# Spreading w_down over 128 partitions, and wo's fourth group in 14 small DMAs, in a one-core decode kernel

## The chip, the core and the metric

One core of a Trainium2 chip runs the whole program. Time is device time in microseconds (us), the median of several executions. Inputs and output are in the chip's main memory; the core computes from its on-chip memory, whose 128 partitions are filled by DMA.

## The reference

One token passes through attention over a cache of 65,536 positions in 32 heads and, beside it, through a gated feed-forward block; a learnt scalar gate mixes the two. All inputs are bfloat16.

```
def _A_ref(x, k_cache, v_cache, wq, wo):        # caches: 1 x 32 x 65536 x 128
    q = (x @ wq).reshape(B, Sq, H, Dh)...        # x: 1 x 1 x 512
    scores = einsum("bhqd,bhkd->bhqk", q, k_cache) * (Dh ** -0.5)
    p = softmax(scores)
    o = einsum("bhqk,bhkd->bhqd", p, v_cache)
    return o...reshape(B, Sq, H * Dh) @ wo       # wo: 4096 x 512
def _B_ref(x, w_gate, w_up, w_down):             # w_down: 1792 x 512
    return (silu(x @ w_gate) * (x @ w_up)) @ w_down
g = sigmoid((x * gate_w).sum(-1))
return g * a + (1 - g) * b
```

The two caches are 1,074 MB of the 1,088 MB that are read.

## The kernel before

**Tiles and ring.** Each head's K and V are cut into four tiles of 16,384 positions, 4 MB each (32 KB on each of 128 partitions). There are 128 K tiles and 128 V tiles; K0, V0 and so on are their numbers here. They share one ring of five buffers (`SLOTS = 5`, tag `big`) with `wq_t`, `gu_t` (w_gate and w_up), `wd_t` (w_down) and, at the end, `wo_t` (the second half of wo). A load into a ring buffer is issued when the last reader of its old content is done.

**Order of work.** The list `steps` pairs the K tile to be scored with the V tile to be summed; V runs four to eight tiles behind K. In each step the queue of SyncE (SP) issues the load of K tile n, then small loads, then the load of V tile v. VectorE multiplies the K tile by the query and folds it from 128 to 16 columns (`products`, L240 and L244). TensorE adds up those columns (`scores`, L254), multiplies the probabilities by the V tile in 32 matmuls (`values`, L302), and projects a finished head by its 128 rows of wo (`project`, L335). The softmax's small steps lie between.

**Feed-forward.** Its three parts run in steps 1 to 3 (`feed_forward_in`, `_mid`, `_out`). w_down is held on 64 partitions with 28 rows of 1 KB each. `hT`, the hidden vector on 128 partitions, is moved to 64 partitions by two matmuls into `h_ps` and a copy to `h2`, and 28 matmuls (L209) then sum into `b_ps`. The ring buffer of `wd_t` is next used by K5, so K5's load waits for the last of these matmuls.

**Who loads w_down and wo.** `load_wd` issues eight DMAs of eight partitions each (L146): two at the start, behind gate_w, and six in step 2, behind K2. wo's first half (heads 0 to 15) comes in four groups of four heads (`load_wo`, L167), each one DMA of 128 partitions by four pieces of 1 KB, into a pool of two buffers. Group 0 is loaded in step 3, groups 1, 2 and 3 in front of V8, V24 and V40. Head 12 is the first to use group 3; it is projected in the step of V52. wo's second half comes behind V127 in five DMAs (`load_wo_end`, L161) of 4, 4, 4, 2 and 2 heads.

**The end.** V126 is loaded in two parts, V127 in five (32, 32, 32, 16 and 16 of 128 columns). After V127's matmuls come the projections of heads 16 to 19, the last head's column (`head_column`, L323) and the projections of heads 20 to 31; then `a_ps` is copied and written out (L413, L414).

Of the kernel before, what the change touches and what calls it, by code (L numbers as in the profile page):

```python
# [8 lines left out]
ACT = mybir.ActivationFunctionType  # L9
ALU = mybir.AluOpType  # L10
AXIS = mybir.AxisListType
P = 128
# [13 lines left out]
def kernel(  # L26
# [14 lines left out]
    nc = tc.nc  # L41
    bf16 = mybir.dt.bfloat16
    f32 = mybir.dt.float32

    _, H, Sk, Dh = A_k_cache.shape
    D = A_x.shape[2]
    F = B_w_gate.shape[1]
    KT = D // P
    FT = F // P
    G = Sk // (NB * P)  # L50
# [6 lines left out]
    consts = ctx.enter_context(tc.tile_pool(name="consts", bufs=1))  # L57
# [3 lines left out]
    wo_pool = ctx.enter_context(tc.tile_pool(name="wo_pool", bufs=2))  # L61
# [3 lines left out]
    psum_m = ctx.enter_context(tc.tile_pool(name="psum_m", bufs=2, space=bass.MemoryType.PSUM))  # L65
# [3 lines left out]
    def big(name):  # L69
        return ring.tile([P, NB * Dh], bf16, name=name, tag="big")  # L70
# [12 lines left out]
    ident_b = consts.tile([P, P], bf16, name="ident_b")  # L83
# [18 lines left out]
    def load(dst, cache, n, name, cuts=(0, NB)):  # L102
        h, g = divmod(n, G)
        t = big(name)
        view = t.rearrange("p (j d) -> p j d", d=Dh)
        src = cache[0, h, g * NB * P : (g + 1) * NB * P, :].rearrange("(p j) d -> p j d", j=NB)
        for a, b in zip(cuts[:-1], cuts[1:]):
            nc.sync.dma_start(out=view[:, a:b, :], in_=src[:, a:b, :])
        dst[n] = view
# [25 lines left out]
    nc.sync.dma_start(out=wgu_sb[:, 1], in_=B_w_up.rearrange("(p t) f -> p t f", t=KT))  # L135
    wd_t = big("wd_t")
    HP = P // 2
    GT = F // HP
    wd_sb = wd_t[:HP, : GT * D].rearrange("p (t n) -> p t n", t=GT)
    wd_rows = B_w_down.rearrange("(p t) n -> p t n", t=GT)  # L140

    def load_wd(*which):
        for i in which:
            lo = (0, 1, 2, 3, 32, 33, 34, 35)[i]
            part = slice(lo, lo + 29, 4)
            nc.sync.dma_start(out=wd_sb[part], in_=wd_rows[part])  # L146

    with nc.allow_non_contiguous_dma(reason="small"):
        nc.sync.dma_start(out=gwT, in_=gate_w.rearrange("(p t) -> p t", t=KT))
# [1 line left out]
    WG = 4  # L151
    wo_tiles = {}

    WH = H // 2
    wo_end = []

    def load_wo_end(cuts):
        t = big("wo_t")[:, : (H - WH) * D].rearrange("p (h n) -> p h n", n=D)
        rows = A_wo[WH * P :, :].rearrange("(h p) n -> p h n", p=P)
        for a, b in zip(cuts[:-1], cuts[1:]):  # L160
            nc.sync.dma_start(out=t[:, a:b, :], in_=rows[:, a:b, :])  # L161
        wo_end.append(t)

    def load_wo(g):
        wo_tiles[g] = wo_pool.tile([P, WG, D], bf16, name="wo_sb")
        rows = A_wo[g * WG * P : (g + 1) * WG * P, :]
        nc.sync.dma_start(out=wo_tiles[g], in_=rows.rearrange("(h p) n -> p h n", p=P))  # L167

    def feed_forward_in():

# [18 lines left out]
    def feed_forward_mid(gu_sb, eg):  # L189
        nc.vector.tensor_scalar_add(eg, eg, 1.0)  # L190
        nc.vector.reciprocal(eg, eg)
        hprod = consts.tile([P, FT], f32, name="hprod")
        nc.vector.tensor_tensor(out=hprod, in0=gu_sb[:, :FT], in1=eg, op=ALU.mult)
        hT = consts.tile([P, FT], bf16, name="hT")
        nc.vector.tensor_tensor(out=hT, in0=hprod, in1=gu_sb[:, FT:], op=ALU.mult)
        xg = consts.tile([P, KT], f32, name="xg")
        nc.vector.tensor_tensor(out=xg, in0=xT, in1=gwT, op=ALU.mult)
        xs = consts.tile([P, 1], f32, name="xs")
        nc.vector.tensor_reduce(out=xs, in_=xg, axis=AXIS.X, op=ALU.add)
        h_ps = psum_m.tile([HP, GT], f32, name="h_ps", tag="misc")  # L200
        for r in range(2):
            nc.tensor.matmul(
                h_ps[:, r * FT : (r + 1) * FT], lhsT=ident_b[:, r::2], rhs=hT, start=True, stop=True
            )
        h2 = consts.tile([HP, GT], bf16, name="h2")
        nc.scalar.activation(out=h2, in_=h_ps, func=ACT.Copy)
        b_ps = psum_m.tile([1, D], f32, name="b_ps", tag="misc")
        for t in range(GT):
            nc.tensor.matmul(  # L209
                b_ps, lhsT=h2[:, t : t + 1], rhs=wd_sb[:, t, :], start=(t == 0), stop=(t == GT - 1)  # L210
            )
        g_ps = psum_m.tile([P, 1], f32, name="g_ps", tag="misc")
        nc.tensor.matmul(g_ps, lhsT=ones_f, rhs=xs, start=True, stop=True)
        eg2 = consts.tile([P, 1], f32, name="eg2")
        nc.scalar.activation(out=eg2, in_=g_ps, func=ACT.Exp, scale=-1.0)
        return b_ps, eg2
# [13 lines left out]
    def products(n, a=0, b=NB):  # L230

        h = n // G
        K = K_tiles[n][:, a:b, :]
        qb = q_bc[:, h * Dh : (h + 1) * Dh]
        q_rep = bass.AP(
            tensor=qb.tensor,
            offset=qb.offset,
            ap=[list(qb.ap[0]), [0, b - a], [1, Dh]],
        )
        yield nc.vector.tensor_tensor(out=K, in0=K, in1=q_rep, op=ALU.mult)  # L240
        half = Dh
        while half > WIDTH:
            half //= 2
            yield nc.vector.tensor_tensor(  # L244
                out=K[:, :, 0:half], in0=K[:, :, 0:half], in1=K[:, :, half : 2 * half],
                op=ALU.add,
            )
# [15 lines left out]
    def row_max(h):  # L263

        m = small.tile([P, 1], f32, name="m")
        nc.vector.tensor_reduce(out=m, in_=S_tiles[h], axis=AXIS.X, op=ALU.max)  # L266
        diag = small.tile([P, P], f32, name="diag")
        nc.scalar.activation(out=diag, in_=ident_f, func=ACT.Copy, scale=m)  # L268
        mT_ps = psum_m.tile([P, P], f32, name="mT_ps", tag="misc")
        nc.tensor.matmul(mT_ps, lhsT=ones_f, rhs=diag, start=True, stop=True)  # L270
        return mT_ps

    def exponentials(h, mT_ps):
        top = small.tile([P, 1], f32, name="top")
        nc.vector.tensor_reduce(out=top, in_=mT_ps, axis=AXIS.X, op=ALU.max)  # L275
        bias = small.tile([P, 1], f32, name="bias")
        nc.scalar.activation(out=bias, in_=top, func=ACT.Copy, scale=-scale)
        P_tiles[h] = ppool.tile([P, NBH], bf16, name="P_sb")
        nc.scalar.activation(  # L279
            out=P_tiles[h], in_=S_tiles[h], func=ACT.Exp, bias=bias, scale=scale,  # L280
            accum_out=rowsum[:, h : h + 1],
        )
        del S_tiles[h]
# [61 lines left out]
    v = 0  # L345
# [9 lines left out]
    for n, v in steps:  # L355
        if n is not None and n > 1:
            load(K_tiles, A_k_cache, n, "K_t")
        if n == 2:
            load_wd(2, 3, 4, 5, 6, 7)
        if n == 3:  # L360
            load_wo(0)
        if v is not None:
            if v % (WG * G) == 2 * G and v // (WG * G) + 1 < WH // WG:
                load_wo(v // (WG * G) + 1)
            load(V_tiles, A_v_cache, v, "V_t", (0, NB) if v < N - 2 else (0, 64, NB) if v < N - 1 else (0, 32, 64, 96, 112, NB))
            if v == N - 1:
                load_wo_end((0, 4, 8, 12, 14, 16))
        if n == 2:
            ff = feed_forward_mid(*ff)
        halves = (0, NB // 2)  # L370
        vector = iter(()) if n is None else products(n)
        if n == 0:
            vector = (i for a in halves for i in products(n, a, a + NB // 2))
        top_of = None
        if n is None:
            top_of = H - 1 if S_tiles else None
        elif n % G == 0 and n > 0:
            top_of = n // G - 1
            vector = (i for a in halves for i in products(n, a, a + NB // 2))
        if top_of is not None:  # L380
            next(vector, None)
            mT_ps = row_max(top_of)
            next(vector, None)
            exponentials(top_of, mT_ps)
        for _ in vector:
            pass
        if n == 1:
            ff = feed_forward_in()
        if n == 3:
            feed_forward_out(*ff)  # L390
        if tot_ps is not None:
            weight(*tot_ps)
            tot_ps = None
        if done is not None:
            head_column(done, head_copy(done))
        if v is not None:
            values(v)
        if top_of is not None:
            tot_ps = top_of, total(top_of)
        if n is not None:  # L400
            scores(n)
        if done is not None and done < WH:
            project(done)
        done = v // G if v is not None and v % G == G - 1 else None
# [40 lines left out]
```

## Time and profile before

| | us |
|---|---|
| median of 3 runs | 2534.66 (2534.63 to 2534.93) |
| the profiled execution | 2534.51 |
| its span (first to last instruction of the program) | 2532.6 |
| 16 DMA engines: share of the span with a packet of the kernel's loads | 99.7% |
| VectorE busy | 2175.5 (86%) |
| TensorE matmul busy | 1742.4 (69%), at a granted clock of 0.749 |
| bytes read | 1087.64 MB, 429 GB/s over the span |

The page gives shares of one execution. Beside it the trace holds a record of every DMA packet, with its start, duration, size and queue, and of every landing, that is, each time one of the 16 DMA engines reports the end of its part of a DMA. A packet is one contiguous piece: 32,768 B for a full K or V tile, 28,672 B for w_down, 1,024 B for wo.

### The profile page before, as it was taken

The page shows a single profiled execution, that of the slowest core. Times are in us where ns is not written, and L with a number is a line of the kernel's source. Part 1 is how long each engine was busy: PE and PEld are TensorE (multiplying, and loading weights), DVE is VectorE, ACT ScalarE, POOL GpSimd, SP SyncE. Part 2 cuts the span into 40 slices and gives each one's busy share as a digit, 9 for nine tenths or more (in the row PEclk, how much of TensorE's full clock was granted, in tenths as well). Part 3 has the DMA queues.
Part 4 walks back from the last instruction along what each step waited for, and adds up shares of the span by engine and source line. Part 5 has one row for each costly group of instructions (what it writes and reads, how often), then busy time and mean ns, then how long its engine had stood idle before and what let it go on. Part 6 is the DMA issues. An engine that isn't in the chain of part 4 may idle for free.

```text
span 2532.6 us, 15260 instructions
## 1 busy us (share of the span) xinstructions
PE 1742.4 (69%) x6738; PEld 712.1 (28%) x6738; DVE 2175.5 (86%) x784; ACT 75.9 (3%) x207; POOL 0.7 (0%) x6
## 2 busy tenths in 40 slices
PE   4677666776677666676776677667666776677679
PEld 2222222222222222222222223222222232222223
DVE  7998888888888999998888888888888888888860
ACT  1000000000000000000000000000000000000000
POOL 0000000000000000000000000000000000000000
PEclk7677777777777676677777777777777777777779
DMA  9999999999999999999999999999999999999998
GB/s 415 433 433 430 433 433 433 432 430 435 432 432 434 431 433 432 432 433 433 432 434 433 432 434 433 432 432 434 432 431 434 433 430 434 434 431 433 434 432 339
DMA packets 42884, 1088.63 MB, mean 430 GB/s; under 512 B 4737, under 2 KB 8834, under 8 KB 9090
## 3 DMA queue, kind: packets, MB, share of 16 engines
q1 hardware_dynamic: 42674, 1087.66, 99.7%
q8 instruction: 53, 0.87, 0.1%
q14 instruction: 13, 0.11, 0.0%
q10 hardware_dynamic: 144, 0.00, 0.0%
HBM read 1087.64 MB, written 0.00 MB: 429 GB/s over the span
## 4 chain that ended last, share of the span: by engine, by line
DMA 68%; PE 22%; DVE 10%; issue 1%; ACT 0%; DVEq 0%; SPq 0%
DMA V_t<-in_A_v_cache_dram 61%; PE O_ps L302 20%; DMA K_t<-in_A_k_cache_dram 5%; DVE K_t L240 5%; DVE K_t L244 5%; PE S_ps L254 1%; DMA wo_t<-in_A_wo_dram 1%; DMA wq_t<-in_A_wq_dram 0%; PE qg_ps L117 0%; DVE m L266 0%; PE oh_ps L323 0%; PE a_ps L335 0%; PE a_ps L227 0%; ACT P_sb L279 0%; DVE top L275 0%
## 5 line engine op out<-in xcount | busy, mean ns | idle before, releaser
L302 PE MATMUL O_ps<-V_t,P_sb 128*4 128x512 bf16 x4096 | 1157.3, 453 | 496.8 <-DMA V_t<-in_A_v_cache_dram 494.3
L240 DVE TENSOR_TENSOR K_t<-K_t,q_bc 128x16384 bf16<-128x16384 bf16 (+1 forms) x160 | 1117.2, 6983 | 254.4 <-DMA K_t<-in_A_k_cache_dram 232.9
L244 DVE TENSOR_TENSOR K_t<-K_t 128x4096 bf16<-128x4096 bf16 (+3 forms) x480 | 1030.9, 2148 | 14.3
L302 PEld LDWEIGHTS <-P_sb 128*4 128x4 bf16 x4096 | 393.9, 97 | 1241.0 <-issue 897.5
L254 PE MATMUL S_ps<-K_t,ident_b 128*128 128x128 bf16 x2048 | 466.0, 394 | 107.0 <-DVE K_t L244 106.9
L254 PEld LDWEIGHTS <-ident_b 128*128 128x128 bf16 x2048 | 227.6, 115 | 330.0 <-issue 140.2
L323 PE MATMUL oh_ps<-ident_f,O_sb 4*128 4x1 f32 x256 | 57.9, 343 | 74.1 <-ACT O_sb L315 74.1
L323 PEld LDWEIGHTS oh_ps<-ident_f,O_sb 4*128 4x128 f32 x256 | 55.2, 314 | 83.7 <-ACT O_sb L315 78.9
L270 PE MATMUL mT_ps<-diag,ones_f 128*128 128x128 f32 x64 | 23.6, 468 | 79.8 <-ACT diag L268 79.8
L268 ACT ACTIVATE diag<-ident_f,m 128x128 f32<-128x128 f32 x32 | 12.8, 401 | 2099.3 <-DVE m L266 2099.3
L317 DVE COPY O_sb<-O_ps 4x256 f32<-4x256 f32 x1 | 0.4, 414 | 52.1 <-ACT O_sb L315 52.1
L270 PEld LDWEIGHTS mT_ps<-diag,ones_f 128*128 128x128 f32 x64 | 14.7, 285 | 95.6 <-ACT diag L268 95.6
L266 DVE TENSOR_REDUCE m<-S_ps 128x1 f32<-128x512 f32 x32 | 21.9, 683 | 7.4 <-PE S_ps L254 7.4
L315 ACT ACTIVATE O_sb<-O_ps 4x512 f32<-4x512 f32 (+1 forms) x32 | 18.1, 566 | 131.0 <-PE O_ps L302 131.0
L279 ACT ACTIVATE P_sb<-S_ps,bias 128x512 bf16<-128x512 f32 x32 | 22.0, 687 | 1.0
L117 PE MATMUL qg_ps<-wq_t,X_bc 128*128 128x512 bf16 x32 | 8.6, 436 | 13.2 <-DMA wq_t<-in_A_wq_dram 13.2
L293 DVE RECIPROCAL recip<-tot_ps 128x1 f32<-128x1 f32 x32 | 5.1, 160 | 12.2 <-PE tot_ps L288 12.2
L209 PE MATMUL b_ps<-wd_t,h 64*1 64x512 bf16 x28 | 12.1, 629 | 4.3 <-DMA K_t<-in_A_k_cache_dram 4.3
L288 PEld LDWEIGHTS tot_ps<-rowsum,ones_f 128*128 128x128 f32 x64 | 9.5, 188 | 14.0 <-issue 14.0
L288 PE MATMUL tot_ps<-rowsum,ones_f 128*128 128x1 f32 x64 | 12.2, 260 | 0.0
L330 ACT ACTIVATE oT<-oh_ps,rg 128x1 bf16<-128x1 f32 x32 | 8.4, 263 | 76.6 <-PE oh_ps L323 76.6
L227 PE MATMUL a_ps<-b_sb,ones_f 1*1 1x512 f32 x2 | 1.9, 1032 | 12.1 <-ACT b_sb L226 12.1
(42 smaller groups left out, 73.8 us busy)
## 6 DMA issues: line engine op xcount, KB each, us to landing
K_t<-in_A_k_cache_dram SPq DMA_DIRECT2D x127, 4096.0 KB, 35.3
V_t<-in_A_v_cache_dram SPq DMA_DIRECT2D x126, 4096.0 KB, 29.1
wq_t<-in_A_wq_dram SPq DMA_DIRECT2D x1, 4096.0 KB
K_t<-in_A_k_cache_dram SPq DMA_DIRECT2D x2, 2048.0 KB, 16.8
V_t<-in_A_v_cache_dram SPq DMA_DIRECT2D x2, 2048.0 KB
V_t<-in_A_v_cache_dram SPq DMA_DIRECT2D x3, 1024.0 KB, 29.4
wo_sb<-in_A_wo_dram SPq DMA_DIRECT2D x4, 512.0 KB, 17.3
gu_t<-in_B_w_gate_dram SPq DMA_DIRECT2D x1, 1792.0 KB
```

Of the source, the lines that this page charges most:

```text
L209: nc.tensor.matmul(b_ps, lhsT=h2[:, t : t + 1], rhs=wd_sb[:, t, :], start=(t == 0), stop=(t == GT - 1))
L240: yield nc.vector.tensor_tensor(out=K, in0=K, in1=q_rep, op=ALU.mult)
L244: yield nc.vector.tensor_tensor(out=K[:, :, 0:half], in0=K[:, :, 0:half], in1=K[:, :, half : 2 * half], op=ALU.add,)
L254: nc.tensor.matmul(S_tiles[h][:, g * NB : (g + 1) * NB], lhsT=ident_b, rhs=K_tiles[n][:, :, c], start=(c == 0), stop=(c == WIDTH - 1),)
L266: nc.vector.tensor_reduce(out=m, in_=S_tiles[h], axis=AXIS.X, op=ALU.max)
L268: nc.scalar.activation(out=diag, in_=ident_f, func=ACT.Copy, scale=m)
L270: nc.tensor.matmul(mT_ps, lhsT=ones_f, rhs=diag, start=True, stop=True)
L279: nc.scalar.activation(out=P_tiles[h], in_=S_tiles[h], func=ACT.Exp, bias=bias, scale=scale, accum_out=rowsum[:, h : h + 1],)
L288: nc.tensor.matmul(tot_ps, lhsT=ones_f, rhs=rowsum[:, h : h + 1], start=True, stop=True)
L302: nc.tensor.matmul(O_tiles[h], lhsT=P_tiles[h][:, g * NB + j : g * NB + j + 4], rhs=V_tiles[n][:, j : j + 4, :], start=(g == 0 and j == 0) ...
L315: nc.scalar.activation(out=O_sb[:, :cut], in_=O_ps[:, :cut], func=ACT.Copy)
L323: nc.tensor.matmul(oh_ps, lhsT=O_sb[:, c * Dh : (c + 1) * Dh], rhs=ident_f[0:4, c : c + 1], start=(c == 0), stop=(c == 3),)
```

## The change

w_down is laid out on 128 partitions with 14 rows each. The eight small DMAs (eight partitions each, the same partitions as before) now carry only the first two rows (`WR = 2`, 2 KB per partition). Two more DMAs follow them in step 2: rows 2 to 13 of all 128 partitions, and rows 0 and 1 of partitions 64 to 127. `hT` is used as it is: the two matmuls and the copy are gone, and `b_ps` is summed by 14 matmuls.

wo's groups 0, 1 and 2 are loaded as before. Group 3 is cut by partitions into 14 DMAs of 3, 5, 6, 7, 9, 10, 11, 12, 13, 14, 15, 16, 4 and 3 partitions (`WP`), one in front of each of V36 to V49.

```diff
     wd_t = big("wd_t")
     HP = P // 2
-    GT = F // HP
-    wd_sb = wd_t[:HP, : GT * D].rearrange("p (t n) -> p t n", t=GT)
-    wd_rows = B_w_down.rearrange("(p t) n -> p t n", t=GT)
+    WR = 2
+    wd_sb = wd_t[:, : FT * D].rearrange("p (t n) -> p t n", t=FT)
+    wd_rows = B_w_down.rearrange("(p t) n -> p t n", t=FT)
 
     def load_wd(*which):
         for i in which:
             lo = (0, 1, 2, 3, 32, 33, 34, 35)[i]
             part = slice(lo, lo + 29, 4)
-            nc.sync.dma_start(out=wd_sb[part], in_=wd_rows[part])
+            nc.sync.dma_start(out=wd_sb[part, :WR, :], in_=wd_rows[part, :WR, :])
...
-    def load_wo(g):
-        wo_tiles[g] = wo_pool.tile([P, WG, D], bf16, name="wo_sb")
-        rows = A_wo[g * WG * P : (g + 1) * WG * P, :]
-        nc.sync.dma_start(out=wo_tiles[g], in_=rows.rearrange("(h p) n -> p h n", p=P))
+    WP = (3, 5, 6, 7, 9, 10, 11, 12, 13, 14, 15, 16, 4, 3)
+
+    def load_wo(g, piece=None):
+        lo, hi = 0, P
+        if piece is not None:
+            lo = sum(WP[:piece])
+            hi = lo + WP[piece]
+        if lo == 0:
+            wo_tiles[g] = wo_pool.tile([P, WG, D], bf16, name="wo_sb")
+        rows = A_wo[g * WG * P : (g + 1) * WG * P, :].rearrange("(h p) n -> p h n", p=P)
+        nc.sync.dma_start(out=wo_tiles[g][lo:hi], in_=rows[lo:hi])
...
-        h_ps = psum_m.tile([HP, GT], f32, name="h_ps", tag="misc")
-        for r in range(2):
+        b_ps = psum_m.tile([1, D], f32, name="b_ps", tag="misc")
+        for t in range(FT):
             nc.tensor.matmul(
-                h_ps[:, r * FT : (r + 1) * FT], lhsT=ident_b[:, r::2], rhs=hT, start=True, stop=True
-            )
-        h2 = consts.tile([HP, GT], bf16, name="h2")
-        nc.scalar.activation(out=h2, in_=h_ps, func=ACT.Copy)
-        b_ps = psum_m.tile([1, D], f32, name="b_ps", tag="misc")
-        for t in range(GT):
-            nc.tensor.matmul(
-                b_ps, lhsT=h2[:, t : t + 1], rhs=wd_sb[:, t, :], start=(t == 0), stop=(t == GT - 1)
+                b_ps, lhsT=hT[:, t : t + 1], rhs=wd_sb[:, t, :], start=(t == 0), stop=(t == FT - 1)
             )
...
         if n == 2:
             load_wd(2, 3, 4, 5, 6, 7)
+            nc.sync.dma_start(out=wd_sb[:, WR:, :], in_=wd_rows[:, WR:, :])
+            nc.sync.dma_start(out=wd_sb[HP:, :WR, :], in_=wd_rows[HP:, :WR, :])
...
-            if v % (WG * G) == 2 * G and v // (WG * G) + 1 < WH // WG:
+            if v % (WG * G) == 2 * G and v // (WG * G) + 2 < WH // WG:
                 load_wo(v // (WG * G) + 1)
+            if 0 <= v - 2 * (WG * G) - G < len(WP):
+                load_wo(WH // WG - 1, v - 2 * (WG * G) - G)
```

## The prediction

> **What bounds the kernel.** I read the page's slices, queues and chain first.
>
> ```profile
> DMA  9999999999999999999999999999999999999998
> ...
> q1 hardware_dynamic: 42674, 1087.66, 99.7%
> q8 instruction: 53, 0.87, 0.1%
> ...
> DMA 68%; PE 22%; DVE 10%; issue 1%; ACT 0%; DVEq 0%; SPq 0%
> ```
>
> The 16 DMA engines never rest, so a change that saves bytes, or shares them out better, is what can move the end. Here the bytes stay; only their shares change. For that a mean over 16 engines is no use. In the trace's packet records each packet starts 3 to 8 ns before the end of the one ahead of it on its engine, and each engine works off SP's loads in order. So I chained the 42,674 packets into 16 rows, one per engine. Steps from one packet to the next: 32,768 B 1209.4 ns, 28,672 B 1058.8, 16,384 B 607.1, 1,024 B 42.35, and 5.85 for the 4-byte packet that ends each DMA's part. They lie on 4.6 ns + 36.77 ps per byte. From K2 to V125 no row has a gap over 0.02 us but at a packet of another queue, and once one of 0.13: no engine ever lacks work.
>
> ```
> end of V127's last packet (us from the span's start), by engine
> 8 engines that carry w_down:    2513.46 2513.54 2513.84 2514.54 2515.93 2519.44 | with fetches: 2522.24 (6)  2523.32 (7)
> 8 engines without w_down:       2506.76 2506.80 | with fetches: 2513.67 (6) 2514.08 (6) 2515.03 (7) 2515.16 (7) 2515.20 (6) 2515.30 (7)
> ```
>
> In brackets are packets of q8, the instruction queue (16 KB each). They go round eight engines in a fixed turn, and each puts its engine back by (2523.32 - 2513.46) / 7 = 1.41 us, or 1.21 on the others. Two engines have both loads, fetches and all of w_down's surplus. The slower one, S below, is the last by 1.08 us, and everything waits for it: a tile is there when its last sixteenth is. That the end hangs on S is seen in VectorE's timeline and the last steps of the chain.
>
> ```profile
> 2436.44 8.69 DVE L240 TENSOR_TENSOR K_t<-K_t,q_bc 128x16384 bf16<-128x16384 bf16 x1 [2.65 <-DMA K_t<-in_A_k_cache_dram]
> ...
> 2504.16 20.87 DMA wo_t<-in_A_wo_dram
> ...
> 2525.07 1.02 PE a_ps L335 x4
> 2526.09 0.98 PE oh_ps L323 x8
> 2527.07 2.69 PE a_ps L335 x12
> ```
>
> VectorE had idled 2.65 us and began K127, the last K tile, 0.09 us after its last landing (2436.34), which is S's. The last landing of wo is at 2529.11, 5.8 us of packets after S's 2523.32, and the matmul that needs it starts at 2529.16.
>
> **The change: w_down.** An engine of the first group had 8 x (1058.8 + 5.85 ns) = 8.52 us. Now it has eight small parts, 8 x (79.9 + 5.85), its eighth of a sixteenth of rows 2 to 13, 8 x 456.4 + 5.85, and four packets of 2 KB: 0.69 + 3.66 + 0.33 = 4.67 us. (79.9 and 456.4 are estimates from the line above; these sizes do not occur before.) So -3.85 us for each of the first group, S among them. The other group had nothing and gets 3.66 + 0.33 = +3.98.
>
> **wo's group 3.** Before, 32 packets on every engine: 32 x 42.35 + 5.85 = 1.36 us. Now a DMA of n partitions gives, I take it, one partition to each of n engines. The row for it: in the packet records w_down's DMAs of eight partitions lie on the same eight engines, one packet each. If those are the lowest-numbered engines each time, engine 0 takes part in all 14 pieces, engine 7 in 8, engine 15 in 1, at 4 x 42.35 + 5.85 = 175 ns each: 2.45 us, 1.40 and 0.18. Against before +1.09, +0.04 and -1.19.
>
> [...]
>
> **Which engine S is.** The turn of the fetches is S, six engines without w_down, the other slow one, and S again. Two neighbours of the first group beside six of the second: engines 6 and 7 (then 8 to 13), or 0 and 1 (with 10 to 15, if the turn runs down). For S the pieces cost +0.04 in the one case, +1.09 in the other. Nothing in the trace decides, so I take the middle for the number and both for the range: S ends 3.85 - 0.04 = 3.81 to 3.85 - 1.09 = 2.76 us earlier, middle 3.3. Who is late next: the second group's latest, 2515.30 + 3.98 + 0.04 = 2519.32 at most, against S's 2519.5 to 2520.6. So S stays the bound, barely.
>
> **SP's queue in step 2.** At the start SP and ScalarE issue eight DMAs at once; the ninth waits for the first, and so on.
>
> ```profile
> SPq L167 <- DMA K_t<-in_A_k_cache_dram: 10.3, 1, 10.3
> ...
> SPq L146 <- DMA xT<-in_A_x_dram: 4.0, 1, 4.0
> SPq L146 <- DMA wq_t<-in_A_wq_dram: 4.0, 1, 4.0
> ```
>
> L167's load is the eighth behind K2 (six of w_down, K3, then it) and was issued at 53.91, 0.49 us behind the end of K2 on S. In the changed order the eighth behind K2 is the second new DMA, and K3 stands behind it: K3's issue moves from 43.20 to about 52.5 (K2 ends on S at 53.42 - 1.96 = 51.46, + 0.49, + one issue of 0.62). From an issue to first packets it takes 1.2 to 2.4 us (wq: 0.74 to 1.95 and 3.13), so K3 starts at 53.7 to 54.9. What hides it is the 3.66 us of rows 2 to 13: an unladen engine is done with w_down at 50.1 + 3.99 = 54.1, S at 51.46 + 4.5 = 55.96. So engines of the second group may idle up to 0.8 us, S none. I take nought for the end and keep 0.8 on the second group for the range: 2519.32 + 0.8 = 2520.1 is still near S.
>
> **The rest, at nothing.** The pieces add 13 issues of about 0.6 us (L146's are 0.62) to SP, in front of V36 to V49, while V's median from issue to landing is 29.1 us. The DMA eight before any of them lies at least five tiles back, whose buffer was already free. Group 3's pool buffer was group 1's, last read in V32's step; its last piece comes with V49 and is needed at V52. Fourteen matmuls of L209 fewer (629 ns), two of L202 and the copy free K5's buffer earlier; K5 was issued 8 us before any engine ran out.
>
> **Sum.** Span 2532.6 - 3.3 = 2529.3; the profiled execution 2534.51 - 3.3 = 2531.2; on the median, 0.15 above it, 2531.35, call it 2531.3. That is 0.13%: within 0.2% of 2534.66, that is 5.07 us, about what a measurement of this kernel can tell from no change. Likeliest case: 2530.85 (S engine 7) to 2531.9 (S engine 0).
>
> **Rivals.** *TensorE sets the tail.* From 2472.6 to the end TensorE has one wait, 1.62 us at 2504.1 for V125. If it cannot start its tail earlier, only that is gained: 2534.66 - 1.62 = 2533.0. For it: the last 25 us are matmuls at 216 ns with slacks of 0.05 to 2 us; a stretch at half clock (it was 0.5 until 2467.1) would double that. Against: the tail hangs on K127's landing, which moves with S. 0.08.
>
> *Odd pieces fall on one engine.* If the split wants a divisor of 16, the rows show no contradiction (eight is one). Then engine 0 alone takes the pieces of 3, 5, 7, 9, 11, 13 and 15 and halves or quarters of the rest: 3+5+3+7+9+5+11+3+13+7+15+1+1+3 = 86 partitions x 4 x 42.35 = 14.6 us, +13.2. If engine 0 is S, the end is 13.2 - 3.85 = 9.4 us later: 2544. Otherwise it decides only where engine 0 comes from behind S: 2513.5 to 2519.4 + 9.4 = 2522.9 to 2528.8 against 2523.3, 2534 to 2540. 0.05.
>
> *Each small DMA costs its engines a pause.* At 1.2 us from issue to packets, unhidden, 14 pieces are 17 us: 2534.66 - 3.3 + 17 = 2548. It would need engines that have run dry between pieces; the records show none in steady state. 0.03. [...]
>
> *More than 5.07 us gained* would need S off the fetches or fewer of them (1.41 each): 0.02.
>
> **Numbers.** Forecast 0.82. Range 2530.4 to 2533.0: down 0.45 from the best end, for the spread of runs and a third of one fetch, up through the tail's rival. Faster by over 0.2%: 0.02. Slower: 0.05 + 0.03 less what of the odd pieces stays inside, 0.07. Within: 0.91.
>
> **What would show it.** Right: packets chained again, S ends V127 at 2519.5 to 2520.6, the second group's engines with fetches close behind, and K3 issued at 52 to 53 behind a wait for K2. Wrong: V127's end on S unmoved, over 8 engines or one with a pile of 1 KB packets between V36 and V49, gaps in the rows, or an end that does not follow S.

## The result and the profile after

The changed kernel takes 2545.61 us (2545.09 to 2546.77, 4 runs) against 2534.64 beside it: ratio 1.0045, 95% interval 1.0032 to 1.0059. It is 11 us slower where 3.3 us less were forecast. The profiled execution took 2546.77, its span 2545.0.

These lines of the profile's page after the change answer to those shown of before; the row of bytes per slice (GB/s) is added.

```profile
span 2545.0 us, 15241 instructions
...
DMA  9999999999999999999999999999999999999998
GB/s 408 429 431 430 430 431 432 429 430 431 432 432 429 427 425 418 427 431 430 432 431 431 431 430 431 433 429 433 431 430 432 431 432 431 432 431 431 431 431 350
...
q1 hardware_dynamic: 43010, 1087.66, 99.7%
q8 instruction: 52, 0.85, 0.1%
...
DMA 70%; PE 22%; DVE 6%; issue 0%; ACT 0%; SPq 0%; DVEq 0%
```

Bytes are the same, the DMA engines are as full as before (99.7%), and the chain has the same shape. So hardly any waiting was added: the engines were busy for longer with the same bytes. The last K tile and the tail show that nearly the whole delay, 11.6 of the 12.4 us between the two spans, is there before the tail (VectorE's timeline, then the chain's last steps; before, VectorE began K127 at 2436.44, and the chain's last DMA step and its last projections began at 2504.16 and 2527.07):

```profile
2448.01 8.69 DVE L240 TENSOR_TENSOR K_t<-K_t,q_bc 128x16384 bf16<-128x16384 bf16 x1 [4.31 <-DMA K_t<-in_A_k_cache_dram]
```

```profile
2516.00 21.15 DMA wo_t<-in_A_wo_dram
2537.20 1.02 PE a_ps L335 x4
2538.22 0.98 PE oh_ps L323 x8
2539.20 2.85 PE a_ps L335 x12
```

Where it builds up is seen when the span is cut at the stage of wo's pieces (V36 to V49). The columns after the times are busy times by engine, the granted clock, the share of DMA and the GB/s. First before, then after:

```profile
700.00:775.00 75.00, 50.12 (x198) 20.63 (x197) 65.04 (x24) 2.12 (x6) 0.00 (x0) 0.77 1.00 433
775.00:1080.00 305.00, 202.19 (x772) 85.20 (x770) 291.92 (x108) 10.19 (x28) 0.00 (x0) 0.70 1.00 432
...
1500.00:2000.00 500.00, 344.00 (x1308) 139.95 (x1305) 434.39 (x156) 14.54 (x41) 0.00 (x0) 0.75 1.00 433
```

```profile
700.00:775.00 75.00, 50.48 (x200) 20.77 (x199) 65.27 (x24) 2.12 (x6) 0.00 (x0) 0.77 1.00 432
775.00:1080.00 305.00, 196.19 (x753) 81.82 (x751) 286.68 (x106) 10.21 (x28) 0.00 (x0) 0.71 1.00 425
...
1500.00:2000.00 500.00, 350.26 (x1315) 140.24 (x1315) 434.19 (x153) 12.70 (x36) 0.00 (x0) 0.75 1.00 431
```

Two things: some GB/s less everywhere, also a thousand microseconds behind the last piece, and a dip among the pieces. The packet records say it more sharply. From 12 us on every undisturbed 32,768 B packet of before lasts 1213 ns (the program's first packets are longer in both kernels). After, the mean is 1213.0 from 12 to 31 us, 1216.8 in 100 to 200 us, 1216.7 in 1500 to 2000, and 1227.3 in 780 to 1080 (packets over 1,400 ns, which stand beside instruction fetches or small packets, left out of these means). The rise is on all 16 engines, and it sets in at about 33 us, in the loads of w_gate and w_up (14,336 B: 535 ns, then 538 to 545), before the first packet of w_down (40.3 us).

### The profile page after: what moved, and what is told of

Its sections match the earlier page's. It is cut to its first block, busy times and chain, and to the rows that moved or that the text cites. A ratio compares the mean times of both kernels' runs of the same rounds, so it can differ in the third digit from the quotient of the medians.

```text
span 2545.0 us, 15241 instructions
## 1 busy us (share of the span) xinstructions
PE 1731.1 (68%) x6722; PEld 707.0 (28%) x6722; DVE 2175.9 (85%) x784; ACT 75.7 (3%) x206; POOL 0.7 (0%) x6
## 3 DMA queue, kind: packets, MB, share of 16 engines
q1 hardware_dynamic: 43010, 1087.66, 99.7%
## 4 chain that ended last, share of the span: by engine, by line
DMA 70%; PE 22%; DVE 6%; issue 0%; ACT 0%; SPq 0%; DVEq 0%
DMA V_t<-in_A_v_cache_dram 63%; PE O_ps L302 21%; DMA K_t<-in_A_k_cache_dram 6%; DVE K_t L240 3%; DVE K_t L244 3%; PE S_ps L254 1%; DMA wo_t<-in_A_wo_dram 1%; PE oh_ps L323 0%; DVE m L266 0%; PE a_ps L335 0%; ACT P_sb L279 0%; PE a_ps L227 0%; PE mT_ps L270 0%; DVE top L275 0%; ACT O_sb L315 0%
## 5 line engine op out<-in xcount | busy, mean ns | idle before, releaser
L323 PEld LDWEIGHTS oh_ps<-ident_f,O_sb 4*128 4x128 f32 x256 | 54.4, 310 | 83.0 <-ACT O_sb L315 78.3
L275 DVE TENSOR_REDUCE top<-mT_ps 128x1 f32<-128x128 f32 x32 | 9.1, 284 | 1.3 <-PE mT_ps L270 1.3
```

The costliest lines, as they stand in the source:

```text
L323: nc.tensor.matmul(oh_ps, lhsT=O_sb[:, c * Dh : (c + 1) * Dh], rhs=ident_f[0:4, c : c + 1], start=(c == 0), stop=(c == 3),)
```

## The experiments

**Is it the kernel, and which part?** First the changed kernel once more, each half of the change alone, and the kernel before.

> The changed kernel once more, unchanged. In its first profile a 32,768 B packet took 1215 to 1222 ns from 33 us on, where the kernel before has 1213 to its end; over some 2,030 packets per engine that is about 8 us. Theory A (the change brings this pace): again 2545 us, and packets of 1213 ns until 33 us, 1215 to 1222 after it. Theory B (the pace is of that execution, from something beside the kernel): packets of 1213 ns and an end near 2531 to 2535 us.

> Only w_down's part of the change; wo's group 3 in one DMA as before. Theory A1 (the new layout of w_down takes away the 8 us by which the first eight engines ran behind the others, and engines in step disturb each other): packets of 1215 to 1222 ns throughout and about +8 - 3.9 = 4 us, 2539 us. Theory A2 (the 14 pieces of wo make the loss): packets of 1213 ns, the slow engine 3.85 us earlier, 2531 us.

> Only wo's part of the change; w_down as before. Theory A1: packets of 1213 ns outside V36 to V49, and a loss of at most the 4 us that V35 to V50 took longer than their packets in the changed kernel: 2535 to 2539 us. Theory A2: the whole loss and more, as w_down's gain is missing: 2545 to 2549 us. By the sum of the prediction alone 2534.8 us.

> The kernel before, with a profile from the same chip as the others. Theory A: packets of 1213 ns to the end and 2534.6 us. Theory B, if what is beside the kernel is still there: packets over 1213 ns here as well, and over 2540 us.

```diff
# w_down only: the change without these lines (group 3 in one DMA again)
-            if v % (WG * G) == 2 * G and v // (WG * G) + 2 < WH // WG:
+            if v % (WG * G) == 2 * G and v // (WG * G) + 1 < WH // WG:
...
-            if 0 <= v - 2 * (WG * G) - G < len(WP):
-                load_wo(WH // WG - 1, v - 2 * (WG * G) - G)
# wo only: before, with WP, load_wo(g, piece) and these lines
-            if v % (WG * G) == 2 * G and v // (WG * G) + 1 < WH // WG:
+            if v % (WG * G) == 2 * G and v // (WG * G) + 2 < WH // WG:
...
+            if 0 <= v - 2 * (WG * G) - G < len(WP):
+                load_wo(WH // WG - 1, v - 2 * (WG * G) - G)
```

| | us | ratio to before, 95% | mean 32 KB packet, 780 to 1080 us | 1500 to 2000 us |
|---|---|---|---|---|
| change again | 2545.62 | 1.0045 [1.003, 1.006] | 1227.3 | 1216.7 |
| w_down only | 2541.71 | 1.0029 [1.0018, 1.0041] | 1217.0 | 1216.8 |
| wo only | 2537.23 | 1.001 [1.0, 1.002] | 1219.3 | 1213.0 |
| before (2534.72 in this batch) | 2534.92, once | | 1213.0 | 1213.0 |

B, a disturbance of one execution, falls: the slower packets come again. So does A2, that the pieces make the whole loss. The pieces make the dip among them and end with it (+2.5 us alone); the w_down half makes the slow packets everywhere, and it alone costs 7 us where it should have gained. A1, that w_down's new shares put the engines in step, was still open, but it has to explain an onset ahead of w_down's first packet.

**What else the w_down half changes.** With `h_ps` and the copy went the tile `h2`. It had 56 bytes on each partition, 64 with padding, and lay ahead of the ring in the on-chip memory. By the sizes of the tiles ahead of it, `wq_t` began at byte 30,976 of each partition (121 x 256) before, and begins at 30,912 (192 beyond a multiple of 256) after; every ring buffer moved with it, since 32 KB is a multiple of 256, and so did wo's buffers and the small tiles, which lie behind the ring. Theory P: this move makes the packets longer. The test puts 64 unused bytes in h2's place, and 192 unused bytes into the kernel before.

```diff
# change and w_down only, with the pad
+    consts.tile([P, 32], bf16, name="pad")
# before, moved
+    consts.tile([P, 96], bf16, name="pad")
# plain w_down, with the pad of 32: no small DMAs, wo as before; in step 2
-            load_wd(2, 3, 4, 5, 6, 7)
-            nc.sync.dma_start(out=wd_sb[:, WR:, :], in_=wd_rows[:, WR:, :])
-            nc.sync.dma_start(out=wd_sb[HP:, :WR, :], in_=wd_rows[HP:, :WR, :])
+            nc.sync.dma_start(out=wd_sb, in_=wd_rows)
```

> The changed kernel with an unused tile of 64 B per partition in the pool of constants. Without it the change puts every later tile 64 B lower, since it no longer has h2 (56 B per partition): the ring's buffers then start 192 B behind a multiple of 256, where before they start on one. Theory P (the place of the ring in a partition sets the packets' pace): 32,768 B packets of 1213 ns throughout, and the end 8 us earlier, 2537 us; what is left over 2531 comes from the pieces between V36 and V49. Theory A1 (engines in step disturb each other): packets of 1215 to 1222 ns and 2545.6 us as without the tile.

> Only w_down's part, with the same 64 B tile. Theory P: packets of 1213 ns, the slow engine 3.85 us earlier, 2531 us, faster than before. Theory A1: 2541.7 us as without the tile.

> The kernel before with an unused tile of 192 B per partition, so that its ring lies 192 B behind a multiple of 256, as in the changed kernel. Theory P: packets of 1215 to 1222 ns from 30 to 50 us on and 8 us more, 2542 to 2543 us. Theory A1: packets of 1213 ns and 2534.7 us.

> w_down in one DMA of 128 partitions behind K2, no small DMAs at all, wo's group 3 in one DMA, with the 64 B tile. Theory P: packets of 1213 ns; each engine has 8 packets of 14,336 B (4.26 us) for w_down, so the slow engine (fetches and half of 8.5 us) gains 4.26 us: 2530.5 us. Theory A1 (all engines in step from the start): packets of 1217 ns or more and 2540 us or later.

| | us | ratio, 95% | 780 to 1080 us | 1500 to 2000 us | V127's last packet ends |
|---|---|---|---|---|---|
| change, pad | 2534.51 | 1.0001 [0.9992, 1.001] | 1220.6 | 1213.0 | 2522.92 |
| w_down only, pad | 2531.81 | 0.9991 [0.9982, 1.0] | 1213.0 | 1213.0 | 2520.84 |
| before, moved by 192 | 2545.07 | 1.0043 [1.0029, 1.0057] | 1217.1 | 1216.8 | 2533.51 |
| plain w_down, pad | 2530.48 | 0.9987 [0.9978, 0.9996] | 1213.0 | 1213.0 | 2519.77 |

(Before: 2534.52 in this batch, V127 2523.32.) P holds in both directions: one unused tile gives the changed kernel 11.1 us back, and one unused tile costs the kernel before 10.5 us, with not one load, wait or matmul changed. P's size was short both times (8 us forecast). A1 falls with it, since w_down's shares are the same with the pad, at 1213.0 ns. An unused tile moves everything that is allocated behind it: these runs don't tell the ring from the rest, nor whether it counts where the loads are written or where the engines read. The same windows, first of before moved by 192, then of the change with the pad:

```profile
700.00:775.00 75.00, 54.79 (x202) 21.75 (x201) 65.28 (x24) 2.12 (x6) 0.00 (x0) 0.73 1.00 432
775.00:1080.00 305.00, 198.13 (x758) 83.04 (x758) 290.80 (x107) 10.20 (x28) 0.00 (x0) 0.70 1.00 431
...
1500.00:2000.00 500.00, 346.94 (x1319) 139.71 (x1317) 434.18 (x152) 12.70 (x36) 0.00 (x0) 0.76 1.00 431
```

```profile
700.00:775.00 75.00, 50.20 (x193) 20.50 (x192) 66.67 (x23) 2.12 (x6) 0.00 (x0) 0.75 1.00 433
775.00:1080.00 305.00, 195.31 (x760) 82.04 (x758) 289.33 (x108) 10.20 (x28) 0.00 (x0) 0.72 1.00 429
...
1500.00:2000.00 500.00, 345.80 (x1309) 140.67 (x1308) 435.84 (x155) 14.82 (x42) 0.00 (x0) 0.75 1.00 433
```

The two effects stand apart: moved, 431 to 432 everywhere and no dip; padded, 433 outside and 429 among the pieces. The GB/s are rounded to whole numbers, and 433 to 431 is 0.5%, so the size is read from times and packets. The moved kernel has 8.1 us more packet time in q1 per engine (2533.22 against 2525.15 in the second run of before), and each of the instruction fetches' 16 KB packets lasts 1064 ns instead of about 930. With seven of them that is 8.1 + 0.9 = 9.0 of the 10.2 us by which V127 ends later. Half of the other 1.2 us is that packets overlap the one ahead less (7.96 us an engine instead of 8.53, summed from 60 to 2500 us); the rest stays without a row.

Plain w_down, one DMA of 128 partitions behind K2 and wo as before, is the fastest version: 4.0 us less than before, and the 95% interval lies below a ratio of 1.

**What makes the pieces cost 2.5 to 2.7 us, and does it matter how far off 256 the ring lies?** With the pad, wo's group 3 was cut in eight DMAs of 8 partitions and one of 64, once with neighbouring partitions in each of the eight, once with every fourth. Packets, sizes and shares are the same in both.

```diff
# the change with the pad; in load_wo, for the piece i (0 to 8, with V36 to V44), cut to the lines on partitions
-            lo = sum(WP[:piece])
-            hi = lo + WP[piece]
# block
+            part = slice(8 * i, 8 * i + 8) if i < 8 else slice(P // 2, P)
# spread
+            lo = (0, 1, 2, 3, 32, 33, 34, 35, 0)[i]
+            part = slice(lo, lo + 29, 4) if i < 8 else slice(P // 2, P)
# before, moved by 64 and by 128
+    consts.tile([P, 32], bf16, name="pad")
+    consts.tile([P, 64], bf16, name="pad")
```

> The changed kernel with the pad, but with wo's group 3 in nine DMAs: eight of 8 neighbouring partitions (0 to 7, 8 to 15, ... 56 to 63, with V36 to V43), then one of partitions 64 to 127 (with V44). Engines 0 to 7 carry eight pieces each, 8 x 175 ns = 1.40, and 0.69 of the last DMA, 2.09 us instead of 1.36: +0.73 for engines 5 and 6. Theory C (a piece of neighbouring partitions sends many engines into the places of one or two engines, whose 32 KB packets then wait): 32 KB packets between V36 and V44 again over 1213 ns in the mean, together 41 us x 8 / 14 = 23 us of excess over 16 engines, 1.5 us each; time 2531.8 + 0.7 + 1.5 = 2534.0. Rival D (it is the count of small DMAs): the same here as in the next kernel. Rival E (only odd pieces do it; eight is a size that goes well): no excess, 2532.5.

> As the kernel before it, but each of the eight pieces takes every fourth partition (0, 4, ... 28; 1, 5, ... 29; and so on), as the small parts of w_down do; sizes, number and engines of the packets are the same. Theory C: no excess beyond some 6 us over all engines, as without pieces; 32 KB packets 1213 to 1214 ns in that stretch; time 2531.8 + 0.7 = 2532.5. Rival D: like the block kernel, about 2534.0. Rival E: 2532.5 for both.

> The kernel before with an unused tile of 64 bytes per partition, so that the ring begins at 64 instead of on a multiple of 256. Theory P in the narrow form (only a multiple of 256 is free of it): about 2545, 32 KB packets 1216.8 ns. Form P64 (what counts is how much of the last or first 256 is missing): 64 and 192 are each other's mirror, still 2545. Form P128 (only what is off a multiple of 128): 2545.

> The same with 128 bytes: the ring begins at 128 beyond a multiple of 256. Narrow form: about 2545 as with 64 and 192. P64: the same or more. P128: 2534.7 and packets of 1213 ns.

Block took 2535.6 us (2535.03 to 2537.55), spread 2533.99 (2533.58 to 2535.23), before 2534.69: ratios 1.0004 [0.9995, 1.0014] and 0.9998 [0.9989, 1.0008]. What 32 KB packets last beyond 1213 ns (those over 1,225 ns), beside each of the small DMAs, summed over the 16 engines, from the packet records:

```
                         pieces by partitions                                   us of excess beside each
change, pad              3 5 6 7 9 10 11 12 13 14 15 16 4 3                      0 .2 .8 .2 2.4 2.2 3.4 5.7 5.2 7.6 7.0 5.9 1.1 .9
block                    8 neighbours x8, then 64 (64 to 127)                    .3 .4 2.1 1.0 2.7 .5 .9 1.2, then 33.8
spread                   8, every fourth x8, then 64 (64 to 127)                 0 0 .6 0 1.2 0 .5 0, then 33.0
w_down only, pad         (group 3 as one DMA of 128)                             .5
```

The eight neighbours cost 9.1 us together, the eight spread ones 2.3, all of that in five packets. Without packets that stand directly behind an instruction fetch it is 7.9 against 1.2. So D, that it is the count of small DMAs, falls, and so does E, that eight is free: it depends on where the partitions lie. C had the direction and not the size (23 us forecast, 9.1 measured): pieces of 4 to 8 neighbours cost little, those of 9 to 16 most. The 14 pieces of the change add up to 42.6 us, 2.7 on an engine in the mean, as much as their price in time (2534.51 - 2531.81). No theory had foreseen the last DMA: 64 neighbouring partitions on 16 engines cost 33 us of excess, two on every engine; beside it 32 KB packets on all 16 engines last up to 2,472 ns, and beside the piece of 14 in the change with the pad all 16 are long at once too, 1,226 to 1,587 ns. By its size, two microseconds on every engine, it would account for the 1.5 to 1.6 us by which both kernels came out over what C gave; no run has the eight pieces without it.

The last DMA is also seen in the row of bytes, at the sixteenth slice of the spread kernel:

```profile
GB/s 410 430 434 432 432 432 435 431 431 435 433 431 433 432 433 417 434 432 433 434 431 434 433 432 432 434 432 433 433 433 432 433 433 432 434 433 432 433 433 355
```

Why neighbours cost more no run shows, and C's cause, waiting at shared places, stays a guess. What was measured is the order: 9.1 us against 2.3, with packets of the same number and size.

Moved by 64 bytes the kernel before takes 2545.01 us (1.0041 [1.0026, 1.0056]), by 128 bytes 2544.59 (1.0039 [1.0024, 1.0054]), with 1216.8 ns a packet in both at 1500 to 2000 us. With 192 (2545.07) that is three offsets with one price: at these offsets the narrow form of P holds, and half of 256 is no better. A move by a whole 256 was not run.

## Why the prediction was wrong

**The sum's base** failed. It took every packet of before at its old duration, 1209.4 ns a step, and added only the packets that change. Under *The rest, at nothing*, the two matmuls of L202 and the copy into `h2` were counted as work that leaves, but not the 64 bytes per partition that leave with them. That is the missing term: +10.5 us (before moved by 192). On 2,032 packets of 32 KB per engine (32,512 / 16), 3.8 ns each are 7.7 us of it.

**wo's group 3** was mis-sized. Its own packets were right: forecast were 175 ns a piece on as many engines as it has partitions, and after, a piece of n partitions shows as n runs of four 1 KB packets, 173 to 177 ns each in the median of a piece. That these are the lowest-numbered engines each time, from which the sum's +1.09 and +0.04 come, no run shows: the records carry no engine's number. There are 4,609 of the 4-byte packets, one at the end of each engine's part, against 4,465: 144 more, which is 2 x 16 for w_down's new DMAs and 128 - 16 for the pieces. So the odd pieces did not fall on one engine. But the term held only what the pieces do on their own engines. What they do to the K and V packets beside them was not in it: +0.04 to +1.09 forecast, +2.5 (wo alone) and +2.7 us (change and w_down only, both with the pad) measured, and 3.9 where the ring is moved as well (2545.62 - 2541.71). The rival of a pause for each small DMA had the sign, at 17 us, and another mechanism, engines that run dry; what the records show is longer packets.

**w_down** held in sign and nearly in size: -3.85 us for S forecast, -2.7 on the median and -2.5 at V127's end (w_down only, pad). In the mean over the engines, half of what is missing has rows, both where K3 comes late. In w_down only with the pad, 32 KB packets have 5.7 us of excess over 16 engines between 54 and 64 us, 0.4 each. And between 53.7 and 57 us engines stood without a packet, 4.7 us over the 16, 0.3 each. Plain w_down, which issues K3 at 39.16 us, has neither there. The excess does not begin beside the six small DMAs (packets from 50.0 us) but at 54.4, with K3's first packets and the DMA of partitions 64 to 127 (from 53.8); no run parts these two.

**Which engine S is**: the pieces tell if each DMA of n partitions takes the n lowest-numbered engines, as the prediction assumed. Then the rows after can be numbered by how many pieces they have, and the fetches go round engines 5, 6 and 9 to 14. The two with both loads are 5 and 6, neither of the pairs that were weighed (6 and 7, 0 and 1). It decided nothing.

**Who is late next** was right, and it caps the gain. Plain w_down takes 8.52 us off S and puts 8 packets of 14,336 B, 8 x 531.7 + 5.85 ns = 4.26 us, on every engine (531.7 is the prediction's line): S at 2523.32 - 4.26 = 2519.06, the second group's latest at 2515.30 + 4.26 = 2519.56. V127 ended at 2519.77.

**SP's queue in step 2** went as forecast: the second new DMA (L361) and K3 behind it waited for K2, and K3 was issued at 52.94 (52 to 53 forecast). Idle engines were put at nothing for the end; in the changed kernel they add up to 1.5 us over all 16, between 53.7 and 55.4 us. SP's timeline after (start, us), and its waits (total, count, mean):

```profile
43.37 0.44 SPq L360 DMA_DIRECT2D wd_t<-in_B_w_down_dram  x1
52.29 0.54 SPq L361 DMA_DIRECT2D wd_t<-in_B_w_down_dram  x1
52.94 0.51 SPq L108 DMA_DIRECT2D K_t<-in_A_k_cache_dram  x1
```

```profile
SPq L361 <- DMA K_t<-in_A_k_cache_dram: 8.5, 1, 8.5
```

**The criterion** named V127's end for S, 2519.5 to 2520.6. It came at 2535.17. Without the move and without the pieces it comes at 2520.84, a quarter of a microsecond outside. Step by step on the moved ring: before 2545.07 (+10.5 against its own batch's before), with w_down's half 2541.71 (-3.4), with the pieces 2545.62 (+3.9), together the 11.0. On the ring in its old place the same two steps are -2.7 and +2.7. The before of the two batches differ by 0.2 us (2534.52 and 2534.72). The forecast's chance of 0.91 for no change was too high because no rival asked what the edit moves without naming it.

One reading of the rival on TensorE's tail was short: besides the wait of 1.62 us there is one of 0.68 us for ScalarE, at 2494.47. It decided nothing.

## What to carry to other kernels

When an edit adds or drops an on-chip tile, however small, work out where everything allocated behind it now begins: here 64 bytes of a helper tile decided 10.5 us, four times what w_down's new layout gained. In a kernel that is bound by its DMA engines, check first whether the undisturbed packets still last what they lasted, before looking for waits. Small DMAs over neighbouring partitions can cost more in the packets beside them than in their own: 42.6 us of excess beside the 14 pieces (their own last some 128 x 175 ns = 22 us), 0.5 beside one DMA of 128 partitions, 2.3 beside eight small ones spread over every fourth.

## What was not expected of the hardware

- In these runs the place where the tiles begin in the on-chip memory sets the pace of the loads: with the ring on a multiple of 256 bytes a 32,768 B packet lasts 1213 ns, at 64, 128 or 192 beyond one 1216.8 in the mean. It is a price per packet more than per byte: in the tail of the moved kernel 16,384 B packets go from 611 to 614.7 ns, 8,192 B from 309 to 314, 4,096 B from 159 to 161, and wo's 1,024 B packets ahead of the tail from 46.0 to 48.7. That is 2 to 5 ns a packet at each of these five sizes. Nor is the price a constant: more than half of those 1,024 B packets (55%) still last 46 ns or less. What makes the packets longer no run shows.
- Up to about 31 us the moved kernels' packets last 1213 ns too. Neither TensorE's first reading of the moved `wq_t` (13.18 us in before moved by 192) nor VectorE's first work on a K tile (18.13) nor TensorE's first sums (35.57) falls together with the onset at 33, and the longer packets stay in the tail, when VectorE is idle (53.83 us without work up to 2535.67, V127's last packet at 2533.51). What sets in there is open.
- One DMA of 256 KB over partitions 64 to 127 made 32 KB packets on all 16 engines last up to twice as long for some 10 us: 33 us of excess beside 256 packets of its own, of 46 to 146 ns each.
